# Moving the sums and subtractions of the full expert groups from GpSimd to VectorE, with a lower priority for the next group's row combinations

## The chip, the cores and the metric

One core of a Trainium2 chip runs the whole program. TensorE (PE) multiplies matrices, VectorE (DVE), ScalarE (ACT) and GpSimd (POOL) do elementwise work, and SyncE (SP) issues most of the DMAs. The metric is the device time of one execution in microseconds (us), lower is better, given as a median of runs. Where a trace is quoted, it is one profiled execution, and its times count from the start of its span.

## The reference

Three stages follow one another: causal attention with a decay, a dense two-layer network, and a mixture of eight experts of which each token uses two. The change lies in the third.

```python
def _moe2_ref(x, w_gate, w_noise, noise, w1, w2):      # x: 2304 x 512
    logits = x @ w_gate                                # 8 experts
    noise_scale = np.log1p(np.exp(x @ w_noise))
    noisy_logits = logits + noise_scale * noise
    top2 = np.argpartition(-noisy_logits, 2, axis=1)[:, :2]
    ...                                                # top2_w: softmax of the two
    for e in range(E):
        for k in range(2):
            mask = top2[:, k] == e
            h = np.maximum(x[mask] @ w1[e], 0.0)       # 512 -> 1024
            out[mask] += top2_w[mask, k, None] * (h @ w2[e])   # 1024 -> 512
```

## The kernel before

**The work.** Every fp32 matrix product is made of three products of rounded halves: a value is split into a high part (a cast on ScalarE) and a low part (value minus high part, on VectorE or GpSimd), and PE multiplies high by high, high by low and low by high. Rows of tokens are first sorted into a table `tab` in DRAM, 640 places for each expert, then taken by ten groups: two small ones (experts 0 and 1, first 256 places), two for the rest of experts 0 and 1 (384 places), and six *full* groups (experts 2 to 7, 640 places, five blocks of 128). The first matrix of a full group is multiplied by a Strassen scheme: two blocks of weights `w1[e, j]`, `w1[e, j+1]` make a pair, and a pair takes seven products of half size instead of eight.

**One full group** is made of these steps, with the lines of the profile:
- `pairprep` (four pairs): DMA of the raw weights (L482), four sums or differences of quarters (`sums`, L493 on VectorE, L494 on GpSimd), then for each of seven quarters a cast on ScalarE (`place`, L488) and a subtraction for the low part (`subtract`, L390 on VectorE, L391 on GpSimd), 256 columns each.
- `wprep` (eight blocks of `w2[e]`): DMA (L411), cast (L446), one subtraction of 512 columns (L390, or on GpSimd L391 in two slices of 256).
- `xtr` and `combos` (five blocks of rows): a 32x32 block transpose on VectorE (L1652), three differences (`diff`, one of 256 and two of 128 columns, L1616 on VectorE, L1617 on GpSimd), and four splits into high and low part (`split`: casts on L1621, three subtractions of 256 and one of 128 columns on L390 or L391). These are the row combinations.
- `strassen` (four pairs): seven products of six matmuls with 320 columns (L1755), three copies from PSUM (`copy`, L1760), three sums (`plus`, VectorE, L1765), four times relu and low part (`out_`, L1775 on ScalarE and L1776 on VectorE).
- `second`: for eight blocks j and five row blocks three matmuls of 512 columns (L1872); then `eout` scales five results (L1854 on ScalarE, L1852 on VectorE) and a GpSimd indirect DMA adds them to the output (L1859, after a small memset, L1858).

**What sets the order.** The kernel is written down by a `Planner`: each step is a thread that yields operations with an estimated cost and a priority (a lower number goes first). The planner keeps a clock for each engine. It takes the operation that can begin first, and among those that can begin within 0.05 us the one with the lowest number. The order in which it takes them is the order of the instructions on each engine and in each DMA queue, and on the chip an engine runs its instructions in that order, each waiting for semaphores. An operation given as `("any", ...)` goes to the engine that is free first by the planner's clock; `ways(kind, ...)` makes such a choice, and since the table `WAYS` is emptied when attention ends, in the expert stage every `subtract` chooses between VectorE and GpSimd. The mark `"port"` tells the planner that an operation on one of these two may not begin while a marked one on the other is running.

**Priorities around the change.** Group number `gi_` has the base number 20000 + 100 gi_, and its products run at this number. Its evacuations (`copy`, `plus`, `out_`) run at 20 below it, its weights of pair j at 30 below it plus 10 j, and its row combinations at `XTP` = 130 below it, which is 30 below the base of the group before. They may begin when the products of the group before the previous one have ended (`mm1_end[gi_ - 2]`), since they overwrite its buffers: that is, when the products of the previous group begin.

**Buffers.** Five slots hold the prepared halves of first weights (a pair takes four), six hold second weights, and raw weights pass through four staging buffers (`stok`). The event `smalls` is set when both small groups have ended.

Of the kernel before, what the change touches and what calls it, by code (L numbers as in the profile page):

```python
# [9 lines left out]
F32 = mybir.dt.float32  # L10
# [194 lines left out]
def dve(n):  # L205
    return (n + 64) / 960
# [34 lines left out]
def tile_attn_mlp_moe(ctx, tc, q, k, v, f, w_in, w_out, gates, noise, w1, w2, out):  # L241
# [152 lines left out]
    def wprep(src, wt, pool, letter):  # L394

        wd = src.dtype != F32
        n = KD * 128
        yield begun
        packed = wd and wt.packed
        if packed:  # L400
            ct = yield ctok
        elif wd:
            ahead = yield pre
        else:
            if wt.late:
                yield placed[letter]
            sl = yield pool
        st = yield stok
        raw = stage(st, [128, n], src.dtype, "wraw")
        dst = raw.rearrange("p (k n) -> p k n", k=KD) if len(src.shape) == 3 else raw  # L410
        yield ("DMA", dma(128 * n * (8 if wd else 4), 4096 if wd else 0), lambda: nc.sync.dma_start(dst, src))  # L411
        val = raw
        if wd:
            pair = raw.bitcast(F32).rearrange("p (n w) -> p n w", w=2)
            low = raw.bitcast(U32).rearrange("p (n w) -> p n w", w=2)[:, :, 0]
            top, val = pair[:, :, 1], pair[:, :, 0]
            ut = yield utok
            g = stg.tile([128, n + 96], F32, name="wg_", tag=f"wg{ut}")[:, 0:n]
            u = stg.tile([128, n], U32, name="wu_", tag=f"wu{ut}")
            gi = g.bitcast(U32)  # L420
            yield ("ACT", act(n, True), lambda: nc.scalar.activation(g, top, AF.Abs))
            yield ("DVE", dve(n / 2), lambda: nc.vector.tensor_scalar(g, g, TINY, None, op0=OP.max), "port")
            yield ("DVE", dve(n / 2), lambda: nc.vector.tensor_scalar(
                u, gi, 3, 0x3FFFFFFF, op0=OP.logical_shift_left, op1=OP.bitwise_and), "port")
            yield ("DVE", dve(n), lambda: nc.vector.scalar_tensor_tensor(
                u, top.bitcast(U32), 0xC0000000, u, op0=OP.bitwise_and, op1=OP.bitwise_or), "port")
            if packed:
                val = w2pool.tile([128, n], F32, name="cw", tag=f"cw{ct}")
            f32 = val.bitcast(U32) if packed else low
            yield ("DVE", dve(n), lambda: nc.vector.scalar_tensor_tensor(  # L430
                f32, low, 29, u, op0=OP.logical_shift_right, op1=OP.bitwise_or), "port")
            yield (utok, ut)
            if packed:
                yield (stok, st)
            sl = yield pool
            if not packed:
                yield (pre, ahead)
        if not wt.late:
            nplaced[letter] += 1
            if nplaced[letter] == NQ * FPQ:  # L440
                yield ("set", placed[letter])
        wt.pool, wt.slot = pool, sl
        hi, lo = [(w3pool if letter == "a" and sl == 4 else wplace[sl]).tile(
            [128, n + (16 if (letter, x, sl) == ("b", "l", NWB - 1) else 0)], FR,
                                  name=f"w{letter}{x}", tag=f"w{letter}{x}{sl}")[:, 0:n] for x in "hl"]
        yield ("ACT", act(n, True), lambda: nc.scalar.copy(hi, val))  # L446
        yield subtract(lo, val, hi.bitcast(F32), n, "wl")
        yield (ctok, ct) if packed else (stok, st)
        wt.hi, wt.lo = hi, lo
        yield ("set", wt.ready)  # L450


    class Pair:

# [7 lines left out]
    def pairprep(srcs, wt, before):  # L462
        yield begun
        yield placed["a"]
        if before:
            yield before.taken
        def slot(i):
            sl = yield watok
            wt.slots.append(sl)
            both = [(w3pool if sl == 4 else wplace[sl]).tile([128, KD * 128], FR, name=f"wa{x}", tag=f"wa{x}{sl}")  # L470
                    for x in "hl"]
            for h in range(2):
                if 2 * i + h < 7:
                    wt.m[2 * i + h] = [x[:, h * 256:(h + 1) * 256] for x in both]

        yield from slot(0)
        st = yield stok
        raw = stage(st, [128, 2 * KD * 128], F32, "wraw")
        got = [event(), event()]
        for i, src in enumerate(srcs):  # L480
            dst = raw[:, i * KD * 128:(i + 1) * KD * 128].rearrange("p (k n) -> p k n", k=KD)
            yield ("go", one_op(("DMA", dma(128 * KD * 128 * 4), lambda d=dst, z=src: nc.sync.dma_start(d, z)), got[i]))  # L482
        a11, a12, a21, a22 = [raw[:, i * 256:(i + 1) * 256] for i in range(4)]
        yield got[0]

        def place(i, val, end):
            hi, lo = wt.m[i]
            yield ("ACT", act(256, True), lambda: nc.scalar.copy(hi, val))  # L488
            yield subtract(lo, val, hi.bitcast(F32), 256, "wl")
            yield ("set", end)  # L490

        def sums(op, d, a, b):
            return ("any", ("DVE", dve(256), lambda: nc.vector.tensor_tensor(d, a, b, op=op), "port"),  # L493
                    ("POOL", pool2(256), lambda: nc.gpsimd.tensor_tensor(d, a, b, op=op), "port"))  # L494

        def filled(i, ends):
            for z in ends:
                yield z
            yield ("set", wt.ready[i])
        ends = [event() for _ in range(7)]  # L500
        yield ("go", place(0, a11, ends[0]))
        yield got[1]
        ut = yield utok
        t = stg.tile([128, KD * 128 + 96], F32, name="wg_", tag=f"wg{ut}")
        s1, s3 = t[:, 0:256], t[:, 256:512]
        t = stg.tile([128, KD * 128], F32, name="wu_", tag=f"wu{ut}")
        s2, s4 = t[:, 0:256], t[:, 256:512]
        made = [event() for _ in range(4)]

        def low():  # L510
            yield sums(OP.subtract, s3, a11, a21)
            yield ("set", made[1])
            yield sums(OP.subtract, s2, a22, s3)
            yield ("set", made[2])
            yield sums(OP.subtract, s4, a12, s2)
            yield ("set", made[3])
        yield ("go", low())
        yield sums(OP.add, s1, a21, a22)
        yield ("go", place(1, s1, ends[1]))
        yield ("go", filled(0, ends[0:2]))  # L520
        yield from slot(1)
        yield ("go", place(2, a12, ends[2]))
        yield made[2]
        yield ("go", place(3, s2, ends[3]))
        yield ("go", filled(1, ends[2:4]))
        yield from slot(2)
        yield made[3]
        yield ("go", place(4, s4, ends[4]))
        yield ("go", place(5, s3, ends[5]))
        yield ("go", filled(2, ends[4:6]))  # L530
        yield from slot(3)
        yield ("set", wt.taken)
        yield ("go", place(6, a22, ends[6]))
        yield ("go", filled(3, ends[6:7]))
        for z in ends:
            yield z
        yield (utok, ut)
        yield (stok, st)
# [989 lines left out]
    M = {}  # L1528
    htok = Tokens(range(4))
    xetok, yotok = Tokens(range(1)), Tokens(range(5))  # L1530
    posttok, freed, small_left, smalls = Tokens(range(1)), event(), [len(EE)], event()
    eids = [c_([128, NBE], f"eids{e}", I32) for e in EE]
    ewab = [c_([128, 2, NBE], f"ewab{e}") for e in EE]
    xftok = Tokens(range(2))
# [1 line left out]
    def group(gi_):  # L1536
# [70 lines left out]
        def combos(b, raw):  # L1607
# [5 lines left out]
            first = bass.AP(tensor=raw.tensor, offset=raw.offset, ap=[list(raw.ap[0]), [64, 2], [128, 2], [1, 64]])  # L1613

            def diff(n, d, x, y):
                return ("any", ("DVE", dve(n), lambda: nc.vector.tensor_tensor(d, x, y, op=OP.subtract), "port"),  # L1616
                        ("POOL", pool2(n), lambda: nc.gpsimd.tensor_tensor(d, x, y, op=OP.subtract), "port"))  # L1617

            def split(n, val, m0, m1, x, end):
                hi, lo = [z[:, m0:m1, :, w].rearrange("p m k c -> p (m k) c") for z in x]  # L1620
                yield ("ACT", act(n, True), lambda: nc.scalar.copy(hi, val))  # L1621
                yield subtract(lo, val, hi.bitcast(F32), n, "wl")
                yield ("set", end)
            ends = [event() for _ in range(4)]
            yield diff(256, T[:, 0:256].rearrange("p (m k c) -> p m k c", k=2, c=64),
# [37 lines left out]
            yield ("set", tev[b])  # L1663
        for (b0_, b1_), z in zip(parts, lev):
            for b in range(b0_, b1_):
                yield ("go", xtr(b, z), prio - XTP)
        if whole:
            for z in lev:
                yield z
# [66 lines left out]
    def strassen(gi_, j, xA, xT, H_, hev, nb, prio):  # L1736
# [33 lines left out]
        def out_(src, w, half, ready, end, sbuf, bi=None):  # L1770
            if ready:
# [2 lines left out]
            v = (src if sbuf else regs[0]).rearrange("p (b c) -> p b c", c=64)  # L1774
            yield ("ACT", act(N, sbuf), lambda: nc.scalar.activation(hh, v, AF.Relu))  # L1775
            yield ("DVE", dve(N), lambda: nc.vector.scalar_tensor_tensor(  # L1776
                hl, v, 0.0, hh.bitcast(F32), op0=OP.max, op1=OP.subtract))
            if bi is not None:
                yield (banks, bi)
            yield ("set", end)  # L1780
# [259 lines left out]
```

## Time and profile before

| what | value |
|---|---|
| time before, median of 3 runs | 1111.69 us (1111.29 to 1112.32) |
| the profiled execution's own time | 1113.31 us |
| its span in the trace | 1111.5 us |
| mean granted TensorE clock over the span | 0.985 |
| first matmul of the full groups' first stage (L1755) | 744.0 us |
| last matmul of the last full group | ends at 1102.3 us |
| busy share of the span: PE, VectorE, ScalarE, GpSimd | 95%, 75%, 53%, 36% |

The span runs from the first to the last instruction on the chip; the execution's own time is 1.8 us longer. The full groups fill the stretch from 744.0 to 1102.4 us, 358.4 us. A group's part of it is counted from its first L1755 matmul to that of the next group. In the rows, a granted clock of 1.00 is 2.4 GHz and 0.50 is 1.2 GHz.

### The profile page before, as it was taken

What the parts mean: (1) busy time and instruction counts of PE and PEld (TensorE: products, weight loads), DVE (VectorE), ACT (ScalarE), POOL (GpSimd) and SP (SyncE); (2) the same over time, 40 slices, a digit from 0 to 9 for tenths busy, and PEclk for the clock granted to TensorE, in tenths of its full rate; (3) what the DMA queues carried; (4) which work ended last, traced back from release to release, by engine and by line L of the source; (5) the groups of instructions that cost most, each with busy time, mean ns of one, the idle gap of its engine ahead of it and who ended that gap; (6) DMA issues with size and microseconds to landing.
All of it is one profiled execution on the core that took longest, in us unless ns stands there. A gap on an engine that the chain in (4) does not pass through costs nothing.

```text
span 1111.5 us, 19723 instructions
## 1 busy us (share of the span) xinstructions
PE 1059.7 (95%) x6700; PEld 934.3 (84%) x6700; DVE 837.5 (75%) x2091; ACT 593.2 (53%) x1525; POOL 394.6 (36%) x579
## 2 busy tenths in 40 slices
PE   9999999999999999999999999997979898999996
PEld 7777888898989898999999779886868787978885
DVE  7899999866786486457888868777877969696551
ACT  7878888844543253333333455564645546464541
POOL 4358334300000000001344223435573827375442
PEclk9999999999999999999999999998989999999998
DMA  8978888577499521000123689764272624534413
GB/s 249 294 217 250 246 244 238 150 213 215 169 265 358 216 76 58 1 1 11 77 78 118 196 245 231 194 169 113 75 163 70 142 93 98 154 72 134 101 33 51
DMA packets 106559, 168.89 MB, mean 152 GB/s; under 512 B 15248, under 2 KB 47760, under 8 KB 106448
## 3 DMA queue, kind: packets, MB, share of 16 engines
q1 hardware_dynamic: 97808, 147.52, 44.3%
q0 software_dynamic: 8640, 20.00, 8.4%
q8 instruction: 55, 0.90, 0.3%
q14 instruction: 56, 0.46, 0.1%
HBM read 118.16 MB, written 49.32 MB: 151 GB/s over the span
## 4 chain that ended last, share of the span: by engine, by line
PE 65%; DVE 19%; ACT 5%; DMA 4%; issue 3%; POOL 1%; SPq 1%; POOLq 0%; DVEq 0%; ACTq 0%
PE h L1105 17%; PE y L1125 16%; PE ye L1872 13%; PE h L1755 9%; PE h L1722 3%; PE O L891 2%; ACT e L730 2%; DVE cw L1616 2%; PE PT L840 2%; DVE hl L1776 1%; DVE wal L390 1%; DVE xf L1652 1%; DVE room L390 1%; DVE e L724 1%; DVE c L1765 1%
## 5 line engine op out<-in xcount | busy, mean ns | idle before, releaser
L1125 PE MATMUL y<-wbh,room 128*128 128x512 f32 x468 | 161.2, 394 | 0.0
L1077 ACT ACTIVATE t<-h 128x256 f32<-128x256 f32 x144 | 55.4, 385 | 116.7 <-PE h L1105 99.2
L1872 PE MATMUL ye<-wbh,hl 128*128 128x512 f32 x288 | 114.3, 397 | 1.7 <-DVE hl L1706 1.7
L1872 PE MATMUL ye<-wbh,hh 128*128 128x512 f32 x288 | 114.8, 399 | 0.0
L1872 PE MATMUL ye<-wbl,hh 128*128 128x512 f32 x288 | 114.0, 396 | 0.0
L1125 PEld LDWEIGHTS y<-wbh,room 128*128 128x128 f32 x468 | 87.8, 188 | 17.6 <-DVE room L390 0.2
L730 ACT ACTIVATE e<-e,m 128x128 f32<-128x128 f32 (+2 forms) x144 | 83.6, 585 | 19.5 <-DVE m L724 19.1
L1081 POOL TENSOR_TENSOR room<-t,onec 128x256 fp32r<-128x256 f32 x13 | 8.5, 654 | 237.2 <-DVE t L1078 128.3
L1125 PE MATMUL y<-wbl,room 128*128 128x512 f32 x234 | 91.4, 391 | 0.0
L1078 DVE SCALAR_TENSOR_TENSOR t<-t,h 128x256 f32<-128x256 f32 x144 | 59.8, 416 | 34.6 <-ACT t L1077 31.9
L1105 PE MATMUL h<-room,wah 128*128 128x256 f32 x576 | 83.2, 282 | 0.0
L1755 PE MATMUL h<-room,wah 128*128 128x320 f32 x336 | 66.7, 321 | 16.0 <-DVE c L1765 10.2
L1105 PEld LDWEIGHTS h<-room,wah 128*128 128x128 f32 x576 | 75.4, 188 | 1.9
L1755 PEld LDWEIGHTS h<-room,wah 128*128 128x128 f32 x336 | 53.7, 192 | 23.9 <-DVE c L1765 14.0
L1859 POOL DMA_INDIRECT out<-yt,ids x36 | 59.3, 1646 | 35.3 <-ACT yt L1854 27.5
L1872 PEld LDWEIGHTS ye<-wbh,hl 128*128 128x128 f32 x288 | 55.1, 191 | 14.5 <-DVE hl L1706 2.1
L1080 ACT CAST room<-t 128x256 fp32r<-128x256 f32 x104 | 42.2, 407 | 46.9 <-DVE t L1078 46.5
L1872 PEld LDWEIGHTS ye<-wbl,hh 128*128 128x128 f32 x288 | 55.2, 192 | 9.8
L840 PE MATMUL PT<-identf,e 128*128 128x128 f32 x400 | 57.7, 278 | 5.9 <-ACT e L730 3.7
L390 DVE TENSOR_TENSOR room<-t,room 128x256 fp32r<-128x256 f32 x103 | 44.3, 432 | 25.1 <-ACT room L1080 23.2
L1872 PEld LDWEIGHTS ye<-wbh,hh 128*128 128x128 f32 x288 | 55.2, 192 | 9.5
L1765 DVE TENSOR_TENSOR c<-h,c 128x320 f32<-128x320 f32 x72 | 34.7, 485 | 37.2 <-PE h L1755 32.7
(678 smaller groups left out, 3100.9 us busy)
## 6 DMA issues: line engine op xcount, KB each, us to landing
wraw<-in_w SPq DMA_DIRECT2D x160, 256.0 KB, 3.1
tab<-padr SPq DMA_DIRECT2D x40, 258.0 KB, 6.2
x<-xo SPq DMA_DIRECT2D x32, 288.0 KB, 3.0
bb<-cneg SPq DMA_DIRECT2D x15, 576.0 KB, 7.2
wraw<-in_w_in SPq DMA_DIRECT2D x16, 512.0 KB, 5.7
wraw<-in_w_out SPq DMA_DIRECT2D x16, 512.0 KB, 6.8
out<-padr SPq DMA_DIRECT2D x23, 256.0 KB, 5.3
xa<-x SPq DMA_DIRECT2D x22, 256.0 KB, 6.5
```

What stands on the lines that cost most here:

```text
L390: return ways(kind, ("DVE", dve(n), lambda: nc.vector.tensor_tensor(dst, a, b, op=OP.subtract), "port"), ("POOL", pool2(n), lambda: slices ...
L730: yield ("ACT", act(n, True, extra=2), lambda: nc.scalar.activation(dst, dst, AF.Exp, bias=m[:, x:x + 1], scale=-1.0, accum_out=sa[:, shar ...
L840: nc.tensor.transpose(ps[:, o:o + 128], w, identf)
L1077: yield ("ACT", act(CH), lambda: nc.scalar.activation(t, h, AF.Tanh, scale=0.851))
L1078: yield ("DVE", dve(CH), lambda: nc.vector.scalar_tensor_tensor(t, t, 1.0, h, op0=OP.add, op1=OP.mult))
L1080: yield ways("gh", ("ACT", act(CH, True), lambda: nc.scalar.copy(gh, t)), ("POOL", pool1(CH), lambda: nc.gpsimd.tensor_tensor(gh, t, onec. ...
L1105: nc.tensor.matmul(h, a[:, kk], z[:, kk], start=(i == 0), stop=(i == len(ops) - 1))
L1125: nc.tensor.matmul(y, a[:, t * 128:(t + 1) * 128], b, start=(n_ == 0 and n == 0), stop=(n_ == FPQ - 1 and n == 2))
L1755: nc.tensor.matmul(regs[r], a[:, kk], z[:, kk], start=(start and n == 0), stop=(n == 5), skip_group_check=True)
L1765: yield ("DVE", dve(N), lambda: nc.vector.tensor_tensor(d, regs[r], d, op=OP.add))
L1859: st = nc.gpsimd.indirect_dma_start(out=out, out_offset=bass.IndirectOffsetOnAxis(ap=ids[:, b:b + 1], axis=0), in_=yt, in_offset=None, com ...
L1872: nc.tensor.matmul(ye[b][0], a[:, b * 128:(b + 1) * 128], w, start=(j == 0 and n == 0), stop=(j == FB - 1 and n == 2))
```

## The change

Five edits, all in the stage of the experts. (1) In `pairprep` the four sums and the seven subtractions are given to VectorE alone. (2) In `combos` the three differences and the four subtractions are given to VectorE alone. (3) In `wprep` the subtraction goes to VectorE if, by the planner's clock, the small groups have ended (`smalls.at` is set), and chooses as before otherwise; for this the event is made earlier in the text. (4) The row combinations of full groups start at 95 below their group's base instead of 130 below it; those of the other groups stay where they were. (5) `out_` is marked as using the port where its input is in SBUF. GpSimd keeps the memsets and the indirect DMAs of the output. No arithmetic is left out or added.

```diff
@@ wprep
-        yield subtract(lo, val, hi.bitcast(F32), n, "wl")
+        if smalls.at is None:
+            yield subtract(lo, val, hi.bitcast(F32), n, "wl")
+        else:
+            yield ("DVE", dve(n), lambda: nc.vector.tensor_tensor(lo, val, hi.bitcast(F32), op=OP.subtract), "port")
...
+    smalls = event()
@@ pairprep
-            yield subtract(lo, val, hi.bitcast(F32), 256, "wl")
+            yield ("DVE", dve(256), lambda: nc.vector.tensor_tensor(lo, val, hi.bitcast(F32), op=OP.subtract), "port")
...
         def sums(op, d, a, b):
-            return ("any", ("DVE", dve(256), lambda: nc.vector.tensor_tensor(d, a, b, op=op), "port"),
-                    ("POOL", pool2(256), lambda: nc.gpsimd.tensor_tensor(d, a, b, op=op), "port"))
+            return ("DVE", dve(256), lambda: nc.vector.tensor_tensor(d, a, b, op=op), "port")
@@ group, combos
             def diff(n, d, x, y):
-                return ("any", ("DVE", dve(n), lambda: nc.vector.tensor_tensor(d, x, y, op=OP.subtract), "port"),
-                        ("POOL", pool2(n), lambda: nc.gpsimd.tensor_tensor(d, x, y, op=OP.subtract), "port"))
+                return ("DVE", dve(n), lambda: nc.vector.tensor_tensor(d, x, y, op=OP.subtract), "port")
...
-                yield subtract(lo, val, hi.bitcast(F32), n, "wl")
+                yield ("DVE", dve(n), lambda: nc.vector.tensor_tensor(lo, val, hi.bitcast(F32), op=OP.subtract), "port")
...
-                yield ("go", xtr(b, z), prio - XTP)
+                yield ("go", xtr(b, z), prio - (XTP if whole or small else 95))
@@ strassen, out_
             yield ("DVE", dve(N), lambda: nc.vector.scalar_tensor_tensor(
-                hl, v, 0.0, hh.bitcast(F32), op0=OP.max, op1=OP.subtract))
+                hl, v, 0.0, hh.bitcast(F32), op0=OP.max, op1=OP.subtract), *(("port",) if sbuf else ()))
```

## Rows read from the trace of the kernel before

**Rows 1.** Page, part 1: busy time, share of the span, instructions.

```profile
PE 1059.7 (95%) x6700; PEld 934.3 (84%) x6700; DVE 837.5 (75%) x2091; ACT 593.2 (53%) x1525; POOL 394.6 (36%) x579
```

**Rows 2.** Stretches: one full group each; us, busy by engine, granted clock, DMA share, GB/s.

```profile
744.00:806.90 62.90, 55.46 (x289) 48.69 (x288) 52.79 (x103) 35.18 (x96) 37.03 (x50) 0.95 0.39 97
806.90:871.00 64.10, 57.24 (x289) 49.90 (x289) 48.99 (x102) 33.40 (x92) 37.80 (x48) 0.92 0.45 107
871.00:933.40 62.40, 57.15 (x290) 49.63 (x289) 51.48 (x103) 33.58 (x90) 33.39 (x44) 0.95 0.43 110
933.40:990.20 56.80, 53.85 (x289) 46.93 (x288) 45.51 (x104) 32.33 (x87) 32.22 (x41) 1.00 0.46 121
990.20:1047.60 57.40, 54.07 (x289) 46.88 (x288) 37.10 (x77) 29.33 (x74) 30.18 (x38) 1.00 0.43 111
1047.60:1102.40 54.80, 53.46 (x290) 46.80 (x288) 26.29 (x46) 21.51 (x55) 26.61 (x36) 1.00 0.32 56
```

**Rows 3.** Chain that ended last, in order of time: start, us, what.

```profile
747.55 1.21 DVE xf L1652 x2
...
752.15 3.89 DVE hl L1776
...
882.77 4.19 DVE wbl L390
...
1069.18 5.28 PE h L1755 x36
...
1076.19 6.16 PE ye L1872 x27
```

**Rows 4.** Waits of PE from 690 us on: us in total, times, longest.

```profile
PE h L1755 <- DVE c L1765: 17.3, 7, 7.0
...
PE ye L1872 <- DVE hl L1706: 1.7, 1, 1.7
```

**Rows 5.** Timeline of VectorE, 876 to 890 us: start, us, what.

```profile
876.53 0.68 DVE L390 TENSOR_TENSOR wbl<-wraw,wbh 128x512 fp32r<-128x512 f32 x1
877.13 0.41 DVE L390 TENSOR_TENSOR xAl<-xf,xAh 128x256 fp32r<-128x256 f32 x1
877.47 0.27 DVE L1616 TENSOR_TENSOR cw<-xf,cw 128x128 f32<-128x128 f32 x1
877.67 0.28 DVE L390 TENSOR_TENSOR xAl<-xf,xAh 128x128 fp32r<-128x128 f32 x1
877.87 0.87 DVE L1765 TENSOR_TENSOR c<-h,c 128x320 f32<-128x320 f32 x2
...
882.69 7.08 DVE L390 TENSOR_TENSOR wbl<-wraw,wbh 128x512 fp32r<-128x512 f32 x1
```

**Rows 6.** Timeline of GpSimd in the same stretch; the last before a pause.

```profile
882.41 2.01 POOL L391 TENSOR_TENSOR wbl<-wraw,wbh 128x256 fp32r<-128x256 f32 x2
...
887.26 1.95 POOL L494 TENSOR_TENSOR wg__11488<-wraw 128x256 f32<-128x256 f32 x2
```

**Rows 7.** GpSimd busy, 744.0 to 1102.4, lines L391, L494 and L1617 in turn.

```profile
744.00:1102.40 358.40, 111.17 (x135) 0.97 0.41 101
...
744.00:1102.40 358.40, 30.70 (x33) 0.97 0.41 101
...
744.00:1102.40 358.40, 12.70 (x19) 0.97 0.41 101
```

**Rows 8.** VectorE by line from 744 us: ns min/median/max, first and last start.

```profile
L390 DVE TENSOR_TENSOR wal<-wraw,wah x42: 402/417/961, 767.2 to 1066.5; 128x256 fp32r<-128x256 f32 x42
...
L1776 DVE SCALAR_TENSOR_TENSOR hl<-c,hh x72: 472/493/3971, 752.1 to 1088.7; 128x320 fp32r<-128x320 f32 x72
...
L1652 DVE STREAM_TRANSPOSE xf<-xe x23: 664/697/705, 747.5 to 990.4; 128x512 f32<-128x512 f32 x23
```

**Rows 9.** Waits of SP's DMA queue from 690 us on.

```profile
SPq L411 <- POOL wbl L391: 25.3, 11, 5.7
```

**Rows 10.** Stretch just ahead of the full groups, columns as in Rows 2.

```profile
680.00:700.00 20.00, 20.00 (x106) 18.35 (x104) 17.41 (x32) 12.03 (x31) 11.89 (x17) 1.00 0.79 192
```

More of the change, by code (lines that the diff above doesn't have):

```diff
@@ L1530, in tile_attn_mlp_moe @@
     xetok, yotok = Tokens(range(1)), Tokens(range(5))
-    posttok, freed, small_left, smalls = Tokens(range(1)), event(), [len(EE)], event()
+    posttok, freed, small_left = Tokens(range(1)), event(), [len(EE)]
     eids = [c_([128, NBE], f"eids{e}", I32) for e in EE]
```

## The prediction

> **What bounds the kernel now.** I read the page's busy shares first: PE 95%, VectorE 75%, GpSimd 36% [rows 1]. An average over three stages decides nothing, so I cut the full groups' stretch into its six groups [rows 2]. A group is always the same work on PE: 168 matmuls of 320 columns and 120 of 512. Where PE runs through, the chain shows 36 of the first in 5.28 us and 27 of the second in 6.16 us [rows 3], so a group costs 168 x 5.28/36 + 120 x 6.16/27 = 24.6 + 27.4 = 52.0 us. The six take 62.9, 64.1, 62.4, 56.8, 57.4 and 54.8 us: losses of 10.9, 12.1, 10.4, 4.8, 5.4 and 2.8 us, 46.4 us together. In the first three the granted clock is 0.95, 0.92 and 0.95, that is, it fell from 2.4 to 1.2 GHz for some us; 62.9 x 0.05 + 64.1 x 0.08 + 62.4 x 0.05 = 11.4 us of the loss at most. The fall comes with the large losses and not in the groups with small ones, so I count it with the holes.
>
> What do the holes wait for? PE's largest wait is for VectorE's sums `c` (L1765), 17.3 us in 7 pieces, the longest 7.0 us [rows 4]; the two longest VectorE pieces of the chain shown are single instructions: a low part of 3.89 us at 752 and a subtraction of 4.19 us at 883, with transposes of the next group's rows ahead of the first [rows 3]. So PE bounds the stage, and VectorE makes its holes at the start of each group, in two ways.
>
> The first way is its order: the next group's row combinations become ready when this group's products begin and stand, by their number, ahead of its evacuations. The second is GpSimd. A subtraction of 512 columns that takes 0.68 us at 876.53 takes 7.08 us at 882.69 [rows 5]; from 882.41 to the one issued at 887.26 GpSimd ran nine sums without a pause [rows 6], and VectorE's next result came when they were over. Over the stage the same 256-column subtraction takes 402 ns at least, 417 in the median, 961 at most, and the low part of 320 columns 472, 493 and 3971 [rows 8].
>
> The Trainium skill, "SBUF — State Buffer", section "Who interferes with whom", says of VectorE with two SBUF inputs and GpSimd that whichever starts second is blocked until the first has finished. By that rule a hold lasts one GpSimd instruction, some 0.7 us here, and the rest of the holds in [rows 3], about 7 us, would have another cause and could stay: the sum below would then end 7 us higher, near 1090. The trace disagrees in the length (nine instructions, not one), so I don't take it.
>
> **What VectorE must do after.** Steps from start to start give the price of an instruction that nothing holds: 512 columns 877.13 - 876.53 = 0.60 us; 256 columns 877.47 - 877.13 = 0.34; 128 columns 0.20 [rows 5]. Two sums of 320 columns take 0.87 together and the last lasts 0.47, so 0.40. A transpose lasts 0.70; less the 0.07 by which a 256-column one lasts longer than its step, 0.63 [rows 5, 8]. A full group with all edits:
> - pair weights, 4 x (4 sums + 7 subtractions) x 0.34 = 15.0
> - second weights, 8 x 0.60 = 4.8
> - row combinations, 5 x (0.63 + 4 x 0.34 + 3 x 0.20) = 12.95
> - `plus` 12 x 0.40 = 4.8, low parts 16 x 0.40 = 6.4
> - two of five results at the 512-column step 1.2, the small index operations 0.5 (estimates)
>
> That is 45.6 us, 88% of PE's 52.0. Six groups make 273.7; seven of the thirty row blocks are done before 744 (23 of the transposes lie behind [rows 8]), 7 x 2.59 = 18.1, and the buffers hold ten quarters with their sums and six blocks, about 15 x 0.34 + 6 x 0.60 = 8.7. So 247 us remain for the stage, against 262.2 that VectorE is busy there now [rows 2].
>
> Yet GpSimd gives away 135 + 33 + 19 = 187 instructions, 154.6 us of its time [rows 7], worth about 60 us on VectorE (160 x 0.34 + 27 x 0.20; at most 187 x 0.34 = 63.6). VectorE's own work now is thus 247 - 60 = 187 us in 262 us of busy time: some 75 us are holds (an estimate from these rows). The move adds 60 us and takes away up to 75. Below, the bound is that the holds stay whole (rival C); above, that all go. I take all, because the two-input instructions of one form show a minimum at the unheld price and a maximum of one or many GpSimd instructions more.
>
> **The other edits.** The lower priority moves 12.95 us of combinations behind this group's evacuations and its weights of the first two pairs (5 above the base, against 20 below it and 30 and 10 below), ahead of its last two pairs (10 and 30 above). They are needed a group later, 52 us, which is their cover. An evacuation then waits for the instruction in progress only, 0.63 us at most. The planner looks at the number only among operations that can begin within 0.05 us; in the bursts at a group's start many can, so it bites there. The `smalls` edit touches weights prepared from about 690 on; VectorE is busy 17.4 of 20 us in the fullest stretch there, with GpSimd's 11.9 beside it [rows 10], and PE waits once, 1.7 us, for a low part [rows 4]. I count these 1.7 as gained; bounds 0 and 1.7. The port mark changes the planner's clock only: nothing.
>
> Queues: a raw weight's buffer is now freed by VectorE where GpSimd freed it, and SP's queue, which stood 25.3 us behind GpSimd's second weights [rows 9], stands behind VectorE's instead. PE's largest wait is for VectorE, not for a load, so I price this at nothing; if VectorE is late, the loads are late next, and rival A shows the cost. A subtraction also waits on VectorE for its cast, with evacuations queued behind; that is part of VectorE's idle time, which rival B prices. GpSimd's queue keeps memsets and scatters alone; the last ones end the kernel as now, 1111.5 - 1102.4 = 9.1 us behind PE.
>
> **The sum.** What remains of the loss is read from the last group: no combinations run beside it, and it loses 2.8 us, though with GpSimd's holds. I add 0.5 for an instruction in progress: 3.3 x 6 = 19.8 us instead of 46.4, 26.6 gained; with 1.7 in front, 28.3. The profiled execution took 1113.3 us (span 1111.5 and 1.8 around it), so 1085.0; the median of the runs lies 1.6 lower: **1083.4 us**. Its own range: with half of the last group's loss everywhere (8.4 us) 1072; with the fifth group's 5.4 us in the first five and 2.8 in the last (29.8 us) 1095.
>
> **Rivals.**
> - *A, weights come late.* In the first half of a group (26 us of PE) VectorE owes two pairs' evacuations 5.6, combinations 12.95, results and indices 1.7, the five subtractions left of the second pair 1.7, and six of the third 2.0: 24 us. That fits only if it idles under 2 us; now it idles 62.9 - 52.8 = 10.1 us in the first group and 10.9 in the third [rows 2], 5 in a half. Then the third pair is 3 us late: 6.3 us of loss in five groups and 3.3 in the last, 34.8; gain 13.3, 1098. For it: the combinations stand ahead of the last pairs' weights. Against: much of the present idling is waiting for a PE that waits itself.
> - *B, VectorE sets the pace: slower.* It works in order; a `plus` that waits for its product holds the weights behind it, and these hold PE. A group then lasts 45.6 plus VectorE's idle time. The first five groups last 60.7 us on average, so it turns slower from 15.1 us of idling a group; the second group idles just that, 64.1 - 49.0. At 18 us: 63.6 us, 5 x 2.9 = 14.5 us slower, 1126. Against: three of the four fullest groups idle 10 to 11.
> - *C, the holds stay.* VectorE's busy time is 47.2 us in the mean of the first five groups; with 10 more for the moved work and the least idling now, 10, a group takes 67.2: 5 x 6.5 = 32.5 us slower, 1144. Against: rows 5, 6 and 8. The Trainium skill, "Perfetto Trace Analysis", section "Optimizing Scalar/DVE Operations", says that where VectorE is saturated, giving work to GpSimd may make sense, and adds that between these two it might not help because of the shared port; the first half of that is this case, the second is the forecast, and the trace bears out the second.
> - *D, nothing comes of it.* The holes lie in the dependencies of a group's first pair (copies, `plus`, low parts in turn), and only their place moves: 1112. Against: the last group has the same chain and loses 2.8 us.
>
> **How the numbers follow.** Forecast 0.58, A 0.22, B 0.09, C 0.03, D 0.05, and 0.03 for still faster than 1072. From 1072 to 1104 lie the forecast and nearly all of A, 0.8. A measurement of this kernel tells about 0.2% (2.2 us) from no change: faster 0.83, same 0.05, slower 0.12.
>
> **What would show it.** Right: GpSimd without sums behind 744; VectorE's 256-column subtractions all near 0.42 us and no instruction over 1 us; its busy time in the stage near 247 us; the transposes of the next group spread over a group instead of bunched at its start; groups of 54 to 57 us at a clock of 1.00. Wrong by A: PE waits for `wah` or `wal` casts and subtractions in the second half of a group. Wrong by B: VectorE idle 15 us and more a group, waiting for PE. Wrong by C: long subtractions while GpSimd only scatters.

## The result and the profile after

The changed kernel takes 1079.01 us (median of 4 runs, 1076.68 to 1080.27) beside 1111.49 us for the kernel before (4 runs). The ratio is 0.9707, 95% interval 0.9687 to 0.9726: 32.5 us less, where 28.3 were forecast. The profiled execution took 1080.27 us, with a span of 1078.4.

Part 1 of the page, as in [rows 1]:

```profile
PE 1049.2 (97%) x6700; PEld 928.2 (86%) x6700; DVE 834.6 (77%) x2278; ACT 593.4 (55%) x1525; POOL 231.3 (21%) x368
```

VectorE runs 187 instructions more (2278 against 2091) and is busy 2.9 us less. GpSimd gives up 211; the 24 beyond 187 are second slices of subtractions of 512 columns, which VectorE does in one instruction. The six groups, with the columns of [rows 2]:

```profile
743.40:799.70 56.30, 55.56 (x299) 48.67 (x298) 53.14 (x147) 36.25 (x97) 6.34 (x8) 1.00 0.51 123
799.70:853.80 54.10, 53.36 (x289) 46.94 (x288) 49.49 (x138) 34.66 (x95) 9.54 (x12) 1.00 0.57 133
853.80:908.10 54.30, 53.42 (x289) 47.01 (x288) 44.55 (x125) 30.96 (x83) 9.17 (x12) 1.00 0.57 127
908.10:961.90 53.80, 52.99 (x289) 47.01 (x288) 45.54 (x126) 32.62 (x87) 8.16 (x12) 1.00 0.56 128
961.90:1016.00 54.10, 53.24 (x290) 47.03 (x289) 42.13 (x112) 30.20 (x79) 8.17 (x12) 1.00 0.44 112
1016.00:1070.00 54.00, 53.05 (x289) 46.81 (x287) 25.95 (x62) 21.62 (x55) 12.36 (x17) 1.00 0.32 57
```

The groups that took 54.8 to 64.1 us take 53.8 to 56.3. Beside PE's 52.0 us a group, 4.3 us are lost in the first and 1.8 to 2.3 in each other, 14.6 together instead of 46.4. Of the first group's 4.3 us, 2.1 are no loss. The planner has put nine matmuls of the group before (L1875, 512 columns) behind this group's first L1758 matmuls, which in the kernel before run ahead of them:

```profile
744.89 0.46 PE L1758 MATMUL h<-room,wal 128*128 128x320 f32 x2
745.19 0.40 PE L1875 MATMUL ye<-wbh,hh 128*128 128x512 f32 x1
...
747.04 0.40 PE L1875 MATMUL ye<-wbh,hl 128*128 128x512 f32 x1
747.27 0.75 PE L1758 MATMUL h<-room,wah 128*128 128x320 f32 x4
```

They take the time from 745.19 to 747.27 us. Without them the first group loses 2.2 us like the others, and the six lose 12.5 us. The granted clock, 0.92 to 0.95 in the first three before, is 1.00 in all, which is 2.4 GHz. GpSimd has only memsets and scatters left in the groups. PE's waits from 690 us on, as in [rows 4], are one line:

```profile
PE h L1758 <- DVE c L1768: 4.4, 7, 0.8
```

VectorE by line, as in [rows 8] (the lines have moved: L494 is the pair weights' subtraction, L1779 the low part, L1655 the transpose):

```profile
L494 DVE TENSOR_TENSOR wal<-wraw,wah x72: 407/419/427, 737.0 to 1043.6; 128x256 fp32r<-128x256 f32 x72
...
L1779 DVE SCALAR_TENSOR_TENSOR hl<-c,hh x72: 473/484/496, 750.1 to 1056.3; 128x320 fp32r<-128x320 f32 x72
...
L1655 DVE STREAM_TRANSPOSE xf<-xe x30: 666/702/715, 686.8 to 971.9; 128x512 f32<-128x512 f32 x30
```

The maxima tell it: 961 ns has become 427, and 3971 has become 496. Minimum and median stay. No instruction got faster; the long ones are gone.

Where did the rest of the difference come from? The span is 33.1 us shorter, the six groups 31.8 (358.4 against 326.6), the tail behind PE 0.7 (9.1 against 8.4). The dense layer's last matmuls started at 617.2 us before:

```profile
L1125 PE MATMUL y<-wbh,room x468: 387/389/486, 137.3 to 617.2; 128*128 128x512 f32 x156
```

and at 620.7 after:

```profile
L1129 PE MATMUL y<-wbh,room x468: 386/389/487, 140.8 to 620.7; 128*128 128x512 f32 x156
```

Up to there nothing was changed; the 3.5 us are the two executions' own difference, already there at the first of these matmuls. From there to the full groups it took 126.8 us (to 744.0) and now takes 122.7 (to 743.4), 4.1 less, of which 2.1 are the nine matmuls that have moved behind that mark. So 31.8 + 4.1 + 0.7 - 3.5 = 33.1.

### The profile page after: what moved, and what is told of

Its sections match the earlier page's. It is cut to its first block, busy times and chain, and to the rows that moved or that the text cites. A ratio compares the mean times of both kernels' runs of the same rounds, so it can differ in the third digit from the quotient of the medians.

```text
span 1078.4 us, 19571 instructions
## 1 busy us (share of the span) xinstructions
PE 1049.2 (97%) x6700; PEld 928.2 (86%) x6700; DVE 834.6 (77%) x2278; ACT 593.4 (55%) x1525; POOL 231.3 (21%) x368
## 4 chain that ended last, share of the span: by engine, by line
PE 72%; DVE 15%; ACT 4%; DMA 3%; issue 2%; POOL 0%; SPq 0%; POOLq 0%; DVEq 0%; ACTq 0%
PE h L1109 17%; PE y L1129 17%; PE ye L1875 14%; PE h L1758 9%; PE h L1725 4%; PE O L895 3%; PE PT L844 2%; ACT e L734 2%; DVE c L1768 1%; PE S L753 1%; DVE wal L494 1%; DVE cw L1620 1%; DMA wraw<-in_w 1%; DVE wbl L450 1%; DVE xf L1655 1%
## 5 line engine op out<-in xcount | busy, mean ns | idle before, releaser
L1875 PE MATMUL ye<-wbh,hh 128*128 128x512 f32 x288 | 113.0, 392 | 0.0
L1875 PE MATMUL ye<-wbh,hl 128*128 128x512 f32 x288 | 112.7, 391 | 0.0
L1875 PE MATMUL ye<-wbl,hh 128*128 128x512 f32 x288 | 112.3, 390 | 0.0
L1758 PE MATMUL h<-room,wah 128*128 128x320 f32 x336 | 64.7, 314 | 2.5 <-DVE c L1768 2.2
L1875 PEld LDWEIGHTS ye<-wbh,hl 128*128 128x128 f32 x288 | 54.1, 188 | 12.1
L1875 PEld LDWEIGHTS ye<-wbl,hh 128*128 128x128 f32 x288 | 54.1, 188 | 9.6
L1875 PEld LDWEIGHTS ye<-wbh,hh 128*128 128x128 f32 x288 | 54.1, 188 | 9.4
L1758 PEld LDWEIGHTS h<-room,wah 128*128 128x128 f32 x336 | 52.6, 188 | 8.6 <-DVE c L1768 6.1
L728 DVE CUSTOM_DVE_ANT_0 e<-S,bb 128x128 f32<-128x128 f32 (+3 forms) x128 | 56.4, 485 | 2.7 <-PE S L757 2.4
```

Source lines behind the costliest of these rows:

```text
L728: nc.vector.tensor_tensor_reduce(dst, src, add, -(D ** -0.5), 3.0e38, OP.add, OP.min, m[:, x:x + 1])
L1758: nc.tensor.matmul(regs[r], a[:, kk], z[:, kk], start=(start and n == 0), stop=(n == 5), skip_group_check=True)
L1875: nc.tensor.matmul(ye[b][0], a[:, b * 128:(b + 1) * 128], w, start=(j == 0 and n == 0), stop=(j == FB - 1 and n == 2))
```

## The experiments

Theory: GpSimd's sums hold VectorE's two-input instructions (a held instruction waits, issued, until GpSimd is through), and these holds make most of PE's holes. Rival: the priority of the row combinations made them. Kernels that are compared ran on one chip with runs of the kernel before, and ratios are to those; for the first four the kernel before took 1117.24 us.

**The engines alone**: the changed kernel with the old priority.

```diff
-                yield ("go", xtr(b, z), prio - (XTP if whole or small else 95))
+                yield ("go", xtr(b, z), prio - XTP)
```

> The changed kernel with the row combinations back at 130 below their group's base: all sums and subtractions on VectorE, old order of priority. If GpSimd's holds on VectorE made most of the holes (my theory), this keeps most of the gain: no VectorE instruction over 1 us in the full groups, 1083 to 1092 us. If the priority of the combinations made them (rival), the holes at the groups' starts come back and it takes 1098 us or more.

It took 1094.27 us, ratio 0.9799 (0.9765 to 0.9833): two thirds of the gain. By its ratio it fits the theory; in us it lies 2 above the range that I gave. PE's largest wait, the first and third group, and VectorE's step to the first `plus` of the first group:

```profile
PE h L1758 <- DVE c L1768: 11.4, 7, 6.1
```

```profile
748.20:808.60 60.40, 54.27 (x289) 48.12 (x288) 53.16 (x152) 36.97 (x102) 7.32 (x8) 0.94 0.42 101
...
862.80:919.10 56.30, 53.96 (x290) 46.98 (x289) 45.60 (x126) 32.63 (x87) 8.43 (x12) 1.00 0.57 127
```

```profile
756.19 0.70 DVE L1655 STREAM_TRANSPOSE xf<-xe 128x512 f32<-128x512 f32 x1
756.82 0.45 DVE L1768 TENSOR_TENSOR c<-h,c 128x320 f32<-128x320 f32 x1
```

Without one held instruction, VectorE still keeps PE waiting 6.1 us at once at the first group's start. From 748.6 to 756.8 us it runs nothing but row combinations, ahead of the first `plus`. The clock falls behind that: the granted clock is 0.59 from 755 to 760 us, where PE works 0.28 us, and 0.73 in the next 5 us. This is the order's share. The six groups take 334.3 us, where the changed kernel takes 324.5 for the same matmuls (326.6 less the nine that moved): 9.8 us.

**The priority alone**: the kernel before with the same line set to 95.

> The kernel before with only the priority of the full groups' row combinations changed (95 instead of 130); sums and subtractions still choose between VectorE and GpSimd. My theory: the holds stay, VectorE keeps single instructions of 2 to 7 us, little is gained: 1098 to 1110 us. Rival (the order made the holes): 1080 to 1092 us.

1115.93 us, ratio 0.9993 (0.9976 to 1.0011): nothing beyond the interval, so 2.7 us of gain at most. The time lies above my range, the reading is the theory's. PE's waits:

```profile
PE h L1755 <- DVE c L1765: 8.6, 9, 1.3
PE h L1755 <- DVE hl L1776: 6.8, 2, 5.8
PE h L1755 <- ACT c L1760: 6.6, 7, 1.6
PE h L1755 <- ACT yt L1854: 5.2, 4, 1.5
PE ye L1872 <- DVE hl L1706: 1.6, 1, 1.6
```

The wait for the sums `c` is half of [rows 4], but a single wait of 5.8 us for a low part has come in, and ScalarE's results are waited for longer: all of PE's waits from 690 us on make 28.8 us, against 28.6 in the kernel before. So the two parts don't add: with GpSimd's sums the lower priority is worth 2.7 us at most, without them some 10 us (0.9799 against 0.9707). The six groups of its profiled execution do take less, 352.6 us instead of 358.4, and the stretch ahead of them more (the first starts at 752.6 us instead of 744.0); without a trace of the kernel before from that chip, how much of either is the order's is not shown. That evacuations which come earlier in VectorE's order then simply become the held ones fits both rows, but it is argued, not shown.

**Sums that nobody needs.** To the changed kernel, six GpSimd sums are added behind each scatter; what all other engines run, and in which order, stays.

```diff
                     in_=yt, in_offset=None, compute_op=OP.add)
+                for _ in range(0 if small else 6):
+                    nc.gpsimd.tensor_tensor(padr[:, 0:256], padr[:, 256:512], padr[:, 256:512], op=OP.add)
```

> The changed kernel with six sums of 256 columns added on GpSimd behind each of its output scatters in the groups from the third on (216 in all, on zeros that nobody reads); the order on all other engines is that of the changed kernel. My theory: nobody needs these sums, yet VectorE is held while they run: VectorE instructions of 2 to 5 us come back at the groups' starts, its busy time in the full groups rises by 40 to 90 us, PE gets holes again, 1092 to 1115 us. Rival (GpSimd only cost time because others waited for its results): within 3 us of the changed kernel. By the one-instruction rule of the Trainium skill's page SBUF - State Buffer no single hold would pass about 1.3 us.

1154.89 us, ratio 1.0348 (1.0327 to 1.0368). The six groups take 382.4 us instead of 326.6, though no instruction needs the results of these sums; the tail takes 26.8 us instead of 8.4, because the sums also stand before the last scatters, and that part says nothing of holds. The second group:

```profile
807.80:873.50 65.70, 57.85 (x289) 49.39 (x288) 61.51 (x137) 34.85 (x95) 29.98 (x41) 0.95 0.48 109
```

VectorE is busy 61.5 us with 137 instructions, where the changed kernel needed 49.5 for 138; over the six groups 325.3 against 260.8. That refutes the rival, that GpSimd costs time only through results that others wait for. Two expectations failed, though. The time lies beyond my range, in part by the tail, and holds of 2 to 5 us did not come. The same subtraction as above has a maximum of 1269 ns:

```profile
L494 DVE TENSOR_TENSOR wal<-wraw,wah x72: 410/421/1269, 737.0 to 1099.5; 128x256 fp32r<-128x256 f32 x72
```

So why 7.08 us in the kernel before [rows 5]? Here all sums write the same place, so each waits for the one before. The pair of runs on how long a hold lasts, below, takes that up.

**Memsets in their place**: the same loop with `nc.gpsimd.memset(padr[:, 0:256], 0.0)`.

> The same as the run with six added sums behind each scatter, but with memsets of 256 columns in their place, which write and read nothing. My theory (what VectorE and GpSimd contend for is the read of a second input): no holds, 1077 to 1082 us, and VectorE's subtractions stay near 0.42 us. Rival (any GpSimd instruction holds VectorE): holds as with the sums.

1091.66 us, ratio 0.9778 (0.9757 to 0.9799), outside of what I expected, but not for VectorE's sake. The second group and the stretch behind PE's end:

```profile
801.90:855.90 54.00, 53.24 (x289) 46.91 (x288) 49.41 (x138) 34.67 (x95) 18.95 (x41) 1.00 0.59 133
...
1072.10:1089.80 17.70, 0.00 (x0) 0.00 (x0) 0.00 (x0) 0.69 (x1) 10.93 (x26) 0.65 0.42 58
```

The group takes 54.0 us as in the changed kernel (54.1), VectorE 49.41 us (49.49), with GpSimd busy 18.95 us beside it instead of 9.5, and the six groups take 326.5 us (326.6). Most of the extra time is the tail, 17.7 us instead of 8.4: I had put memsets ahead of the last scatters. Another 2.2 us lie ahead of the full groups. GpSimd's memsets, which read nothing, hold nobody.

**Parts given back, and the priority lowered further**, beside the changed kernel itself on the same chip.

> The changed kernel itself, so that the other runs of this call have it on the same chip: ratio to the kernel before near 0.971.

1079.62 us, ratio 0.9705 (0.9680 to 0.9730).

```diff
@@ wprep: the second weights choose again
-        if smalls.at is None:
+        if True:
```

> The changed kernel with the smalls edit undone: the second weights' subtractions (and those of the third and fourth group) choose between VectorE and GpSimd as before. My theory: 48 instructions of 512 columns may go to GpSimd as 96 slices, some of them do, and each holds VectorE: 3 to 12 us more than the changed kernel. Rival (only the pair weights and combinations mattered): within 2 us of it.

1096.18 us, ratio 0.9843 (0.9820 to 0.9866): 16.6 us more than the changed kernel, more than I expected; the six groups of its profiled execution take 344.6 us, 18.0 more. GpSimd needs few sums for that: in the six groups it runs 116 instructions instead of 73.

```diff
@@ combos: differences and subtractions choose again
             def diff(n, d, x, y):
-                return ("DVE", dve(n), ...)
+                return ("any", ("DVE", dve(n), ...), ("POOL", pool2(n), ...))
...
-                yield ("DVE", dve(n), ...)    # split
+                yield subtract(lo, val, hi.bitcast(F32), n, "wl")
```

> The changed kernel with the row combinations' differences and subtractions choosing between VectorE and GpSimd again (priority 95 kept); weights on VectorE alone. My theory: 35 instructions of a group can go to GpSimd, fewer than half do, and they bring holds back in the bursts at a group's start: 4 to 15 us more than the changed kernel. Rival (it was the weights' sums alone that held VectorE): within 2 us of it.

1106.59 us, ratio 0.9948 (0.9930 to 0.9966): 27.0 us more, four fifths of the gain gone, with the weights still on VectorE. Its VectorE and GpSimd near 753 us:

```profile
753.17 4.79 DVE L494 TENSOR_TENSOR wal<-wraw,wah 128x256 fp32r<-128x256 f32 x1
```

```profile
752.83 1.31 POOL L391 TENSOR_TENSOR xTl<-cw,xTh 128x256 fp32r<-128x256 f32 x1
753.51 1.73 POOL L391 TENSOR_TENSOR xAl<-xf,xAh 128x256 fp32r<-128x256 f32 x2
...
755.03 2.65 POOL L391 TENSOR_TENSOR xTl<-cw,xTh 128x256 fp32r<-128x256 f32 x3
```

A subtraction of 0.42 us takes 4.79: it ends at 757.96, after the last of GpSimd's sums (757.68). But holds are not all of this run: PE's largest wait is for ScalarE's copies (11.2 us in 9 pieces), and ScalarE itself waited 11.6 us, in 18 pieces, for GpSimd's differences `cw`, a wait of 3.3 us in all in the kernel before. What each of the two costs was not separated. Each part alone can thus spoil half of the gain or more; 16.6 + 27.0 is more than the 33.2 us of the whole, and the planner's order changes with each as well.

```diff
-                yield ("go", xtr(b, z), prio - (XTP if whole or small else 95))
+                yield ("go", xtr(b, z), prio - (XTP if whole or small else 60))
```

> The changed kernel with the row combinations at 60 below their base, behind all weights of the group in progress. Rival A of the prediction (weights of the last pairs late behind the combinations) would gain 3 us or more from it. My theory now: PE loses only 2 us a group in the changed kernel and none to weights, so no change within 2 us.

1079.35 us, ratio 0.9698 (0.9676 to 0.9721), the changed kernel's time. With the combinations behind all weights of the group in progress nothing is gained, so weights are not late behind them: rival A of the prediction is out.

**How long a hold lasts.** Twelve unused sums of 128 columns behind each scatter of the third to ninth group: once with outputs that go round four places, so that no sum need wait for the one before, once all into one, so that each must.

```diff
+                for i in range(0 if small or gi_ == len(groups) - 1 else 12):
+                    nc.gpsimd.tensor_tensor((padr[:, 0:128], padr[:, 128:256], padr[:, 256:384],
+                                             nzs.rearrange("p n e -> p (n e)")[:, 0:128])[i % 4],
+                                            padr[:, 384:512], padr[:, 384:512], op=OP.add)
```

The other kernel has `padr[:, 0:128]` as the output of all twelve.

> The changed kernel with twelve sums of 128 columns added on GpSimd behind each output scatter of the third to ninth group (372 in all, unused results), their outputs going round four places, so that one need not wait for the one before. Theory (VectorE gets in only where GpSimd pauses between two instructions): they run without a pause, and single VectorE instructions are held for several of them, 2 to 6 us, as in the kernel before. By the rule of one instruction (Trainium skill, SBUF - State Buffer): no hold over 1 us.

> The same twelve sums, all into one place, so that each waits for the one before and GpSimd pauses some 0.08 us between two. Theory: VectorE gets in at each pause, every two-input instruction is held for one sum at most, none over 1 us, and the time is well below that of the run with sums that needn't wait. By the rule of one instruction: the same time and holds in both runs.

The sums that needn't wait: 1178.49 us, ratio 1.0582 (1.0550 to 1.0614). Those that wait for each other: 1111.38 us, ratio 0.9998 (0.9987 to 1.0010). The same number of sums of the same size costs 67 us more when they don't wait for one another. The waiting ones are not free either: beside them the six groups take 359.6 us instead of 326.6. VectorE in the first of the two:

```profile
893.55 4.81 DVE L494 TENSOR_TENSOR wal<-wraw,wah 128x256 fp32r<-128x256 f32 x1
898.28 0.61 DVE L494 TENSOR_TENSOR wal<-wu__11298,wah 128x256 fp32r<-128x256 f32 x1
```

and GpSimd there:

```profile
893.60 1.67 POOL L1866 TENSOR_TENSOR padr<-padr 128x128 f32<-128x128 f32 x3
894.67 0.95 POOL L1866 TENSOR_TENSOR nzs<-padr 128x128 f32<-128x128 f32 x1
...
897.52 1.08 POOL L1866 TENSOR_TENSOR nzs<-padr 128x128 f32<-128x128 f32 x1
```

Each sum starts before the one ahead of it has ended, and the subtraction that was issued with the first ends at 898.36, when the last of the twelve is nearly through. By line, in this kernel (L1768 is `plus`, with one input in PSUM):

```profile
L494 DVE TENSOR_TENSOR wal<-wraw,wah x72: 411/422/4807, 739.7 to 1142.8; 128x256 fp32r<-128x256 f32 x72
...
L1768 DVE TENSOR_TENSOR c<-h,c x72: 445/484/503, 752.0 to 1154.5; 128x320 f32<-128x320 f32 x72
```

and in the one whose sums wait:

```profile
L494 DVE TENSOR_TENSOR wal<-wraw,wah x72: 407/427/655, 737.1 to 1077.2; 128x256 fp32r<-128x256 f32 x72
```

4807 ns against 655. Where each sum waits for the one before, the trace has 0.08 us between the end of one and the start of the next; in the other kernel it has no such pause within a row. The outputs' places differ between the two as well; that was not varied by itself. A `plus`, which reads PSUM and one place of SBUF, is never held, not even in the first. The Trainium skill, "SBUF — State Buffer", section "Who interferes with whom", says that VectorE contends with GpSimd where it has two inputs in SBUF and GpSimd reads SBUF, and not where GpSimd only writes: both hold here (503 ns for `plus`, 54.0 us a group beside memsets). The Trainium skill, "SBUF — State Buffer", section "Summary: rules for kernel authors", says that the second waits until the first has finished. The run with dependent sums agrees (655 ns at most), the run with independent ones does not: there a VectorE instruction waits for the whole row of twelve (4807 ns).

**The small groups' weights too**: `if smalls.at is None` becomes `if not wt.late`, so that all weights of the experts are VectorE's alone.

> The changed kernel with the weights of the small groups given to VectorE alone too (32 subtractions of 512 columns, prepared from about 600 us on): a candidate that may beat the changed kernel. If the holds cost PE time there as in the full groups, 2 to 5 us less than the changed kernel, near 0.967 of the kernel before; if VectorE, which also evacuates the dense layer there, is then the later one, the same or some us more.

1080.88 us, ratio 0.9697 (0.9675 to 0.9719): the same as the changed kernel within the interval. It does not beat it.

## Why the prediction was right, point by point

- *PE bounds the stage, at 52.0 us a group.* Right: the groups came down to 53.8 to 56.3 and none went under.
- *The holds go, all of them.* Right: the pair weights' subtraction keeps within 407 to 427 ns, no VectorE instruction in the full groups passes 1 us, and unused sums bring the holds back. That GpSimd's sums alone do it, without anyone needing their results, is shown. The size was too large: the moved work of about 60 us and a busy time that went from 262.2 to 260.8 make 61 us of holds (an estimate), not 75.
- *VectorE's work, 247 us.* It was busy 260.8. The step that was mis-sized is the work done ahead of the full groups: 25 sets of row combinations, 45 of the 48 second-weight subtractions and 253 of the 264 pair-weight operations lie behind 743.4 us, where 23, 42 and 249 were counted, some 8 us at the prices of the prediction. The other 6 us were not taken apart; a price from start to start leaves out the end of an instruction that no other follows at once, which is one part. It cost the forecast nothing, since VectorE keeps 3 to 12 us of idle time in each of the first five groups.
- *3.3 us of loss a group, 19.8 in all.* Measured 12.5 (14.6 with the nine matmuls that moved in). The 2.8 us of the last group had holds in them too: it now loses 2.0, and the groups with combinations beside them hardly more. This term is 7.3 us too large, more than the whole difference between forecast and result; the 3.5 us by which this execution came later to the dense layer hide part of it.
- *1.7 us before the full groups.* Measured 4.1, less the 2.1 of the nine matmuls 2.0; PE's one wait there of 1.7 us is gone. In the profile of the changed kernel's second set of runs the same stretch (618.3 to 742.5) takes 124.2 us instead of 122.7, so the size is uncertain by more than 1 us.
- *The priority.* The prediction counted it together with the engines. The runs put it at 2.7 us at most while GpSimd sums, and some 10 us without them.
- *The combinations spread over a group.* Hardly: in the trace after, the five transposes for the second full group lie between 742.8 and 765.6 us, those for the third between 791.1 and 811.6, around the second group's start at 799.7. It is enough that evacuations go first.
- *Rivals.* A is out by the run with a priority of 60; B by the idle times; C by the maxima; D by the time. The rule of one instruction, which I had set aside for the 7.08 us of [rows 5], holds only where GpSimd pauses.

What stays open: what makes 27 us of the combinations' 35 instructions a group, since there the planner's order moved and ScalarE waited for GpSimd as well.

## What to carry to other kernels

Before giving half of VectorE's sums to GpSimd, look at the maximum of one VectorE form beside its minimum: 402 to 961 ns, or 0.68 and 7.08 us, is a sign that one engine holds the other, and that the help is paid for by the engine that was to be helped. Here 187 instructions worth 60 us came back to VectorE and made it no busier. And try such a change together with the order that it was tuned with: the lower priority alone was worth 0.24% at most, and some 0.9% once the holds were gone.

## What the runs showed of the hardware

In these traces a VectorE instruction with two inputs in SBUF waits not for one GpSimd sum but for as many as follow without a pause: 4.81 us for twelve sums of 128 columns, 7.08 us for nine of 256. Where each sum depends on the one before, with 0.08 us between two, VectorE gets in between: 655 ns at most for the same subtraction. A `plus`, with one input in PSUM, is not held in either case (503 ns at most). Scatters and memsets on GpSimd held nothing: in the changed kernel's full groups, where they are all that it runs, the subtraction stays within 427 ns.
